# The first pair's q and k in one transfer each, put in order on the chip

## The chip, the cores and the metric

The kernel runs on one NeuronCore of a Trainium2 chip. The metric is the device time of one execution in microseconds, inputs and outputs in HBM; the median of three runs counts. A second, profiled execution gives the trace that is read here.

## The reference

The program is three blocks in a row, all in float32: causal attention over 2 x 12 heads with 448 tokens and a head size of 64, a channel-mixing FFN whose weights come as float64, and a gated FFN with a convolution over the hidden features, also with float64 weights. The change touches only the loading of the first q and k:

```python
scores = scale * np.matmul(q, k.transpose(0, 1, 3, 2))      # q, k, v: (2, 12, 448, 64)
scores = np.where(causal_mask, -1e9, scores)
attn = softmax(scores)                                       # max subtracted, + 1e-9 below
x = np.matmul(attn, v)                                       # heads side by side: (2, 448, 768)
x = rwkv_ffn(x, mu_k, mu_r, w_k, w_v, w_r)                   # token shift, relu^2, sigmoid gate
out = conv_ffn(x, w_in, conv_w, w_out)
```

## The kernel before, in words

Attention goes by pairs of heads, 12 jobs (class `Job`). A pair's raw tile has, on partitions 0 to 63, q and, on 64 to 127, k: seven chunks of 64 tokens, partition p of chunk c holding token 64 c + p, both heads side by side (`half`, line 210). So a partition's tokens lie 64 apart in HBM and each transfer of one head is 448 pieces of 256 B. `Lk` (lines 300 to 306) issues the q halves on SP and, for pair 0 and for pairs from 4 on, the k halves: pair 0's from ScalarE's queue. For pairs 1 to 3 GpSimd issues k (`Lp`). Pair 0's second q half is issued by GpSimd ahead of everything else (line 212).

`kqT` (line 322) turns the chunks on TensorE: 7 transposes for q and 7 for k, chunk c to columns 64 c to 64 c + 63 of a PSUM bank. `kC` copies the two banks to SBUF as qT and kT. `sc` multiplies them to scores, `red` subtracts the mask and takes the row extreme on VectorE, `exp` is on ScalarE, `norm` mostly on GpSimd, `T_`, `C` and `V` bring the probabilities to v.

The order on TensorE, VectorE, ScalarE and GpSimd is written out by hand in the string `ORDER` (line 527): each token such as `0:kqT` or `0:kC.q/v` issues its instructions in program order on its engines, a letter behind the slash naming the engine. Transfers on SP keep the order in which the tokens issue them. `W0` and `W*n` are dummy matmuls of 128 x 128 on a tile of ones (`keep_warm`, line 589); each shows as two passes in the trace. `sm:L` loads small parameters on SP (`mu_k`, `mu_r`, `conv_w`); `sm:a` takes the absolute value of the raw `conv_w` on ScalarE, the first ACTIVATE of the kernel; `sm:n` does four small VectorE steps. `w1:L` loads the first slice of a weight matrix.

Raw weights have two buffers (`raws`, line 111). `turn` takes the next free buffer and puts it at the end of the list again: the dummy operand `warm` takes the first one, so that the list stands at the second when slice 1 asks for one. A buffer is written again only when all readers of the tile that had it are done.

Later stages (`xr_products`, the pk, pv and ph products) follow in `ORDER` and in a stretch that a planner orders; they read nothing that the change touches.

Of the kernel before, what the change touches and what calls it, by code (L numbers as in the profile page):

```python
# [9 lines left out]
F32 = mybir.dt.float32  # L10
# [9 lines left out]
def kernel(  # L20
# [18 lines left out]
    nc = tc.nc  # L39
    B, H, S, D = q.shape  # L40
    P = 128
    WT = 3 * P
    LO = P // 2
# [34 lines left out]
    def copy(eng, out_, in_):  # L78
        (nc.vector.tensor_copy if eng == "v" else nc.scalar.copy)(out_, in_)  # L79
# [31 lines left out]
    raws = Slots(wp, "wraw", 2, [P, NF * P], I64)  # L111
# [6 lines left out]
    def in_order(ins):  # L118
        if pinned[0]:
            tc.keep_in_program_order(ins)  # L120
# [86 lines left out]
    first_qk = qks.get(0, "rqk_0")  # L207

    def half(x, b, h):
        return x[b, h].rearrange("(c p) d -> p c d", p=LO)  # L210

    nc.gpsimd.dma_start(out=first_qk[:LO, :, 1], in_=half(q, 0, 1))
    warm = raws.turn("warm").bitcast(F32)[:, :P]
    nc.vector.memset(warm, 1.0)
    ident = smp.tile([P, P], F32, tag="ident", name="ident", bufs=1)
    make_identity(nc, ident)

# [2 lines left out]
    for r in (slice(0, LO), slice(LO, P)):  # L220
        nc.gpsimd.affine_select(
            out=mask[r, MAIN:], in_=mask[r, MAIN:], compare_op=ALU.is_ge,
# [9 lines left out]
    def home(tag):  # L232
        return act if tag in early else late[0]

    def big(tag, name):
        return home(tag).tile([P, 2, NT], F32R, tag=tag, name=name)
# [8 lines left out]
    def width(t):  # L245
        return t.stop - t.start
# [4 lines left out]
    def bank(key, uses):  # L251
        tag = free.pop(0)
        t = ps.tile([P, 512], F32, tag=tag, name=key, bufs=1)
        held[key] = [tag, t, uses]
        return t

    def used(key):
        h = held[key]
        h[2] -= 1
        if not h[2]:  # L260
            free.append(h[0])
        return h[1]

    NQ = S // LO
# [21 lines left out]
    class Job:  # L286
# [12 lines left out]

        def Lk(self):  # L300
            self.raw = first_qk if self.i == 0 else qks.get(self.i, self.name("rqk"))
            for j in range(2):
                if self.i or j == 0:
                    in_order(nc.sync.dma_start(out=self.raw[:LO, :, j], in_=half(q, self.b, 2 * self.hp + j)))
            if self.i not in (1, 2, 3):
                self.k_half(nc.sync if self.i else nc.scalar)

        def Lp(self):
            self.k_half(nc.gpsimd)
# [12 lines left out]
        def kqT(self, _):  # L322
            t = self.raw
            pt = {n: bank(self.name(n), 1) for n in "qk"}
            for c in range(NQ):
                for n, r in (("q", slice(0, LO)), ("k", slice(LO, P))):
                    nc.tensor.transpose(
                        pt[n][:, c * LO:(c + 1) * LO], t[r, c].rearrange("p h d -> p (h d)"), ident[r, r]
                    )
            qks.put(self.i)  # L330

        def kC(self, eng, n):
# [125 lines left out]
    def products(out_, w, x, t, n, c):  # L458
        o = slice(c * P, c * P + P)
        mm3(out_, w[0][:, 0, o], w[0][:, 1, o], x[c][:, 0, t], x[c][:, 1, t], c == 0, c == n - 1)  # L460
# [21 lines left out]
    def first_steps(s):  # L482

        if s == "L":
            t = act.tile([P, 4 * P], F32, tag="U2", name="small")
            small["m"] = mr = t[:2 * NC, :P]
            in_order(nc.sync.dma_start(out=mr[:NC], in_=mu_k.rearrange("(c p) -> c p", p=P)))
            in_order(nc.sync.dma_start(out=mr[NC:], in_=mu_r.rearrange("(c p) -> c p", p=P)))
            small["r"] = cr = t[:3 * NF, 2 * P:]
            in_order(nc.sync.dma_start(out=cr.bitcast(I64), in_=conv_w.rearrange("t (f p) -> (t f) p", p=P)))  # L490
            small["c"] = t[:3 * NF, P:2 * P]
        elif s in "an":
            for x in "a" if s == "a" else "bcde":
                narrow(x, small["c"], small["r"].bitcast(I32))
        elif s == "T":
            pm = bank("small", 1)
            nc.tensor.transpose(pm[:, :2 * NC], small["m"], ident[:2 * NC, :2 * NC])
            nc.tensor.transpose(pm[:, P:P + 3 * NF], small["c"], ident[:3 * NF, :3 * NF])
        else:
            pm = used("small")  # L500
            nc.vector.tensor_copy(mu[:, :2 * NC], pm[:, :2 * NC])
            nc.vector.tensor_scalar(mu[:, 2 * NC:4 * NC], mu[:, :2 * NC], -1.0, 1.0, ALU.mult, ALU.add)
            nc.vector.tensor_copy(cw, pm[:, P:P + 3 * NF])

    class Slice:
# [19 lines left out]
                wcs.put(e)  # L525

    ORDER = """
        W0 W*2 0:Lk sm:L sm:a 0:kqT W*2 0:kC.q/v sm:n W*1 0:kC.k/a 0:sc.2 0:red.2 0:exp.2 0:red.3 1:Lk 1:Lp 2:Lk
        2:Lp pads 0:red.0 1:kqT 0:sc.1 1:kC.q/v 1:kC.k/a 1:sc.2 0:red.5 0:red.1 1:sc.1 0:exp.0 0:red.6 0:exp.3
        0:exp.5 0:red.4 1:red.3 0:exp.1 1:red.2 3:Lk 3:Lp 0:exp.6 4:Lk 0:exp.4 2:kqT 1:red.5 2:kC.q/v 2:kC.k/a  # L530
        w1:L 0:rec 0:norm.6/p 0:norm.1/p 1:red.0 1:exp.5 0:norm.5/p 1:exp.0 0:norm.0/p 0:norm.4/p 1:red.6
# [57 lines left out]
    def keep_warm(n):  # L589
        for _ in range(n):  # L590
            nc.tensor.matmul(ones[:, :P], warm, warm, start=True, stop=True)

    def xr_products(e, b, c):
        if c == 0:
            bank(f"pr{e}_{b}", 1)
        t = PART[b]
        products(held[f"pr{e}_{b}"][1][:, :width(t)], [slices[e].t], xr, t, NC, c)
        xr_done[e] += 1
        if xr_done[e] == B * NC:
            whls.put(e)  # L600

    def keep_sr(e, b, eng):
        if e not in sr:
            sr[e] = home(f"U{e}").tile([P, NT], F32, tag=f"U{e}", name=f"sr{e}")
        t = PART[b]
        copy(eng, sr[e][:, t], used(f"pr{e}_{b}")[:, :width(t)])

    def xk_step(x, s, eng):
        b, c = divmod(x, NC)
        if s == "H":  # L610
            mix_h(xk[c], mixed[c][:, b], b, eng)
        else:
            mix_l(xk[c], mixed[c][:, b], b, eng)
# [4 lines left out]
    def issue(token):  # L618
        what, _, eng = token.partition("/")
        if what == "W0":  # L620
            keep_warm(7)
        elif what == "pads":
            for z in pads:
                nc.gpsimd.memset(z, 0.0)
        elif what == "Wend":
            used("W")
        elif what[:2] == "W*":
            keep_warm(int(what[2:]))
        elif what == "act2":
            actx.close()  # L630
            late.append(ctx.enter_context(tc.tile_pool(name="act2", bufs=1, reuse_waits="tile")))
            for c in (1, 4, 0, 2, 5, 3):
                xk[c] = big(f"X{c}", f"xk{c}")
            for e in (4, 5, 3):
                sr[e] = home(f"U{e}").tile([P, NT], F32, tag=f"U{e}", name=f"sr{e}")
        elif what[0] == "E":
            f, b = divmod(int(what[1:]), B)
            t = PART[b]
            pk_banks[f, b] = bank(f"pk{f}_{b}", 1)[:, :width(t)]
            for c in range(NC):  # L640
                products(pk_banks[f, b], [slices[NE + f].t], [xk[i] for i in range(NC)], t, NC, c)
        elif what[:2] == "pr":
            xr_products(*(int(y) for y in what[2:].split(".")))
        elif what[:2] == "sr":
            keep_sr(*(int(y) for y in what[2:].split(".")), eng)
        else:
            who, op = what.split(":")
            if who == "sm":
                first_steps(op)
            elif who[0] == "w":  # L650
                slices[int(who[1:])].step(op, eng)
            elif who[0] == "k":
                xk_step(int(who[1:]), op, eng)
            else:
                op, *a = op.split(".")
                job = jobs[int(who)]
                if op in ("Lk", "Lp", "Lv"):
                    getattr(job, op)()
                else:
                    getattr(job, "T_" if op == "T" else op)(eng, *a)  # L660

    ET = mybir.EngineType
    with tc.manual_schedule(engines={ET.PE, ET.Activation, ET.DVE, ET.Pool}):
        for token in ORDER.split():
            issue(token)
# [58 lines left out]
    for f in range(NF):  # L724
# [3 lines left out]
        for t, pk in pks:  # L728
            a = mslots.turn(f"a{f}")[:, :t.stop - t.start]
# [8 lines left out]
    for e in range(NE):  # L738
# [3 lines left out]
        for t, pv in token_mm(f"pv{e}", w, k2, e == 0):  # L742
            a = mslots.turn(f"xv{e}")[:, :t.stop - t.start]
# [358 lines left out]
```

## Time and profile before

| | |
|---|---|
| median of three runs | 353.47 us (353.36 to 353.78) |
| profiled execution | 353.09 us |
| its span, first to last instruction | 351.3 us |
| TensorE busy | 344.4 us, 98% |
| VectorE busy | 308.8 us, 88% |
| ScalarE busy | 223.4 us, 64% |
| GpSimd busy | 96.0 us, 27% |

Times within the trace count from the first instruction. In the trace PE is TensorE's matmul and PEld its weight load, DVE is VectorE, ACT ScalarE, POOL GpSimd and SP SyncE; a q behind a name is its instruction queue, where a transfer's issue stands. TensorE's ends are modelled, so that neighbours overlap in the timeline.

### The profile page before, as it was taken

What the parts mean: (1) busy time and instruction counts of PE and PEld (TensorE: products, weight loads), DVE (VectorE), ACT (ScalarE), POOL (GpSimd) and SP (SyncE); (2) the same over time, 40 slices, a digit from 0 to 9 for tenths busy, and PEclk for the clock granted to TensorE, in tenths of its full rate; (3) what the DMA queues carried; (4) which work ended last, traced back from release to release, by engine and by line L of the source; (5) the groups of instructions that cost most, each with busy time, mean ns of one, the idle gap of its engine ahead of it and who ended that gap; (6) DMA issues with size and microseconds to landing.
All of it is one profiled execution on the core that took longest, in us unless ns stands there. A gap on an engine that the chain in (4) does not pass through costs nothing.

```text
span 351.3 us, 7223 instructions
## 1 busy us (share of the span) xinstructions
PE 344.4 (98%) x2682; PEld 307.0 (87%) x2682; DVE 308.8 (88%) x645; ACT 223.4 (64%) x502; POOL 96.0 (27%) x153
## 2 busy tenths in 40 slices
PE   8899999999999999999999999999999999999995
PEld 7678787888888898988898999998888999999995
DVE  3999999999999988889988998888997999888731
ACT  3999999999300067777795354346657868757501
POOL 8577988973814000000000000000000000368000
PEclk9999999999999999999999999999999999999999
DMA  7955693531422424554627244544241200389523
GB/s 184 242 131 133 139 259 67 144 118 32 150 90 91 129 64 168 179 211 145 214 93 238 90 135 136 174 139 138 90 125 56 90 2 0 67 141 221 115 90 135
DMA packets 60320, 45.33 MB, mean 129 GB/s; under 512 B 31608, under 2 KB 59036, under 8 KB 60284
## 3 DMA queue, kind: packets, MB, share of 16 engines
q1 hardware_dynamic: 56140, 39.90, 37.4%
q0 software_dynamic: 3216, 4.74, 7.2%
q8 instruction: 21, 0.34, 0.4%
q10 hardware_dynamic: 928, 0.23, 0.3%
q14 instruction: 15, 0.12, 0.1%
HBM read 38.17 MB, written 2.75 MB: 117 GB/s over the span
## 4 chain that ended last, share of the span: by engine, by line
PE 88%; DVE 4%; ACT 4%; POOL 2%; issue 1%; POOLq 0%; ACTq 0%
PE pk L66 17%; PE pv L66 17%; PE pr L66 13%; PE A L66 7%; PE po L418 4%; PE B L66 4%; PE s L348 3%; ACT p L370 3%; PE c L66 2%; PE D L66 2%; DVE e L361 2%; PE Yb L390 1%; PE ph5l L66 1%; PE ph4l L66 1%; PE ph6l L66 1%; PE ph7l L66 1%
## 5 line engine op out<-in xcount | busy, mean ns | idle before, releaser
L925 POOL DMA_DIRECT2D s<-g x12 | 12.7, 1179 | 191.3 <-ACT st L87 185.1
L370 ACT ACTIVATE p<-e,st 128x128 f32<-128x128 f32 (+6 forms) x84 | 43.0, 528 | 1.8 <-DVE st L361 1.8
L72 POOL TENSOR_SCALAR p<-p,st 128x384 f32<-128x384 f32 (+6 forms) x70 | 36.4, 538 | 14.3 <-DVE st L361 4.4
L361 DVE CUSTOM_DVE_ANT_0 e<-s,mask 128x128 f32<-128x128 f32 (+6 forms) x84 | 31.7, 413 | 0.5 <-PE s L348 0.5
L730 ACT ACTIVATE a<-pk 128x384 f32<-128x384 f32 (+1 forms) x16 | 8.5, 534 | 35.8 <-PE pk L66 35.8
L418 PE MATMUL po<-pt,v 128*64 128x128 f32 (+4 forms) x384 | 23.8, 277 | 0.0
L348 PE MATMUL s<-kT,qT 64*64 64x448 f32 (+6 forms) x336 | 22.5, 386 | 0.6 <-ACT p L370 0.3
L418 PEld LDWEIGHTS po<-pt,v 128*64 128x64 f32 x384 | 20.0, 137 | 3.4 <-ACT pt L79 0.2
L845 DVE SCALAR_TENSOR_TENSOR cv<-hT,cw,cv 128x448 f32<-128x448 f32 x32 | 21.5, 679 | 1.3 <-ACT cv L842 1.3
L348 PEld LDWEIGHTS s<-kT,qT 64*64 64x64 f32 x336 | 14.5, 132 | 6.6 <-ACT kT L79 0.6
L370 ACT ACTIVATION_READ_ACCUMULATOR p<-e,st 128x1 f32 x84 | 18.2, 217 | 0.0
L87 ACT ACTIVATE x<-xv 128x512 fp32r<-128x512 f32 (+1 forms) x12 | 6.8, 577 | 9.0 <-DVE xv L744 8.9
L91 DVE TENSOR_TENSOR k<-a,k 128x384 fp32r<-128x384 f32 (+1 forms) x16 | 9.8, 619 | 1.6 <-ACT k L87 1.6
L849 ACT ACTIVATE cv<-cv 128x448 f32<-128x448 f32 x16 | 9.1, 571 | 3.2 <-DVE cv L845 3.2
L842 ACT ACTIVATE cv<-hT,cw 128x448 f32<-128x448 f32 x16 | 10.7, 668 | 0.5 <-DVE g L91 0.3
L851 DVE TENSOR_TENSOR cv<-cv,hT 128x448 f32<-128x448 f32 x16 | 9.9, 619 | 1.2 <-ACT cv L849 1.2
L1037 ACT ACTIVATE o<-A 128x384 f32<-128x384 f32 x3 | 1.5, 491 | 14.7 <-PE A L66 14.6
L66 PE MATMUL pv<-k,wv0hl 128*128 128x512 f32 (+1 forms) x48 | 9.9, 364 | 0.0
L925 POOL DMA_DIRECT2D wo6raw<-g x8 | 8.8, 1153 | 3.9 <-ACT wo6raw L950 3.9
L66 PE MATMUL pv<-k,wv2hl 128*128 128x512 f32 (+1 forms) x48 | 9.8, 363 | 0.0
L66 PE MATMUL pv<-k,wv5hl 128*128 128x512 f32 (+1 forms) x48 | 9.8, 363 | 0.0
L66 PE MATMUL pv<-k,wv3hl 128*128 128x512 f32 (+1 forms) x48 | 9.8, 363 | 0.0
(520 smaller groups left out, 1102.9 us busy)
## 6 DMA issues: line engine op xcount, KB each, us to landing
rqk<-in_q_dram SPq DMA_DIRECT2D x23, 112.0 KB, 3.2
v<-in_v_dram SPq DMA_DIRECT2D x24, 96.0 KB, 3.2
s<-g POOLq DMA_DIRECT2D x12, 192.0 KB, 4.2
rqk<-in_k_dram SPq DMA_DIRECT2D x16, 112.0 KB, 3.0
wo6raw<-g POOLq DMA_DIRECT2D x8, 192.0 KB, 4.7
wv0raw<-in_moe_w_v_dram SPq DMA_DIRECT2D x1, 1024.0 KB, 4.6
wv1raw<-in_moe_w_v_dram SPq DMA_DIRECT2D x1, 1024.0 KB, 4.7
wv2raw<-in_moe_w_v_dram SPq DMA_DIRECT2D x1, 1024.0 KB, 4.8
```

The lines of the kernel that those rows point to most:

```text
L66: nc.tensor.matmul(ps_out, x, y, start=first and i == 0, stop=last and i == 2, skip_group_check=more,)
L72: nc.gpsimd.tensor_scalar(out_, in_, s, 1.0, ALU.mult, ALU.mult)
L91: e.tensor_tensor(out_, x, f32(h), ALU.subtract)
L348: nc.tensor.matmul(held[self.name(f"s{f}")][1][h, o:z], qT[r, i * LO:(i + 1) * LO], kT[r, :(i + 1) * LO], start=True, stop=True,)
L361: nc.vector.tensor_tensor_reduce(t[:, :w], used(self.name(f"s{f}"))[:, o:z], mask[:, S - w:], -SCALE, 3e38, ALU.add, ALU.min, self.st[:, 0 ...
L370: nc.scalar.activation(p[:, :w], self.s[i][:, :w], AF.Exp, bias=self.st[:, 0, i:i + 1], scale=-1.0, accum_out=self.st[:, 1, i:i + 1],)
L418: nc.tensor.matmul(self.T["po"][j * D:(j + 1) * D, 1 + i * LO - z:1 + (i + n) * LO], self.v[:, kc, j], self.T["pt"][:, a - z:a + n * LO], ...
L842: nc.scalar.activation(a, x[:, 0:S], AF.Copy, scale=cw[:, f:f + 1])
L845: nc.vector.scalar_tensor_tensor(a, x[:, j:S + j], cw[:, j * NF + f:j * NF + f + 1], a, ALU.mult, ALU.add)
L849: nc.scalar.activation(a, a, AF.Sigmoid)
L851: (nc.gpsimd if eng == "p" else nc.vector).tensor_tensor(a, a, hc, ALU.mult)
L925: nc.gpsimd.dma_start(out=dst, in_=f32(x), accum_op=ALU.add)
```

## The change

Pair 0's q and k come in one transfer each, both heads together, q from SP and k from ScalarE. Partition p gets the seven tokens 7 p to 7 p + 6, which lie in a row in HBM, so that a piece is 7 x 64 x 4 = 1792 B. They land in a staging tile with the heads one behind the other. VectorE copies chunks 0 to 3 and ScalarE chunks 4 to 6 to the raw tile, heads side by side. Chunk c then holds the tokens 7 p + c, and the transposes of pair 0 write to every seventh column from c on, so that the banks hold the tokens in order. GpSimd's transfer at the start is gone. `0:Lk` stands first in `ORDER`; there are 5 dummy matmuls in `W0` instead of 7, and a `W*2` ahead of the transposes is gone. The staging tile takes its turn in the raw-weight buffers, behind `warm`.

```diff
-    nc.gpsimd.dma_start(out=first_qk[:LO, :, 1], in_=half(q, 0, 1))
     warm = raws.turn("warm").bitcast(F32)[:, :P]
     nc.vector.memset(warm, 1.0)
+    stage = raws.turn("stage").bitcast(F32)[:, :2 * S].rearrange("p (j c d) -> p j c d", j=2, c=S // LO)
...
         def Lk(self):
             self.raw = first_qk if self.i == 0 else qks.get(self.i, self.name("rqk"))
+            if self.i == 0:
+                self.whole_rows()
+                return
             for j in range(2):
-                if self.i or j == 0:
-                    in_order(nc.sync.dma_start(out=self.raw[:LO, :, j], in_=half(q, self.b, 2 * self.hp + j)))
-            if self.i not in (1, 2, 3):
-                self.k_half(nc.sync if self.i else nc.scalar)
+                in_order(nc.sync.dma_start(out=self.raw[:LO, :, j], in_=half(q, self.b, 2 * self.hp + j)))
+            if self.i > 3:
+                self.k_half(nc.sync)
+
+        def whole_rows(self):
+            for x, r, e in ((q, slice(0, LO), nc.sync), (k, slice(LO, P), nc.scalar)):
+                in_order(e.dma_start(
+                    out=stage[r].rearrange("p j c d -> p j (c d)"),
+                    in_=x[0, :2].rearrange("j (p c) d -> p j (c d)", p=LO),
+                ))
+            for e, cs in (("v", slice(0, 4)), ("a", slice(4, NQ))):
+                copy(e, self.raw[:, cs], stage[:, :, cs].rearrange("p j c d -> p c j d"))
...
-                    nc.tensor.transpose(
-                        pt[n][:, c * LO:(c + 1) * LO], t[r, c].rearrange("p h d -> p (h d)"), ident[r, r]
-                    )
+                    cols = slice(c * LO, (c + 1) * LO) if self.i else slice(c, S, NQ)
+                    nc.tensor.transpose(pt[n][:, cols], t[r, c].rearrange("p h d -> p (h d)"), ident[r, r])
...
-        W0 W*2 0:Lk sm:L sm:a 0:kqT W*2 0:kC.q/v sm:n W*1 0:kC.k/a 0:sc.2 0:red.2 0:exp.2 0:red.3 1:Lk 1:Lp 2:Lk
+        0:Lk W0 sm:L sm:a 0:kqT W*2 0:kC.q/v sm:n W*1 0:kC.k/a 0:sc.2 0:red.2 0:exp.2 0:red.3 1:Lk 1:Lp 2:Lk
...
         if what == "W0":
-            keep_warm(7)
+            keep_warm(5)
```

## Rows read from the trace of the kernel before

**Rows 1.** Window 20 to 89 us: busy us per engine (instructions), granted clock, DMA share, GB/s

```profile
20.00:89.00 69.00, 68.17 (x1123) 56.62 (x1119) 67.59 (x217) 68.49 (x205) 52.45 (x82) 1.00 0.51 132
```

**Rows 2.** Timeline, 0 to 5 us: start, us, engine, line, operation, tiles, count, idle before

```profile
0.74 0.72 SPq L304 DMA_DIRECT2D rqk<-in_q_dram  x1
0.74 1.66 ACTq L313 DMA_DIRECT2D rqk<-in_k_dram  x2
1.06 4.21 PE L591 MATMUL W<-warm 128*128 128x128 f32 x18 [1.06 <-DVE warm L214]
1.29 0.91 POOL L212 DMA_DIRECT2D rqk<-in_q_dram  x1 [0.85 <-POOLq L1086]
...
2.43 1.28 ACT L140 ACT_TABLE_LOAD   x1 [2.43 <-issue]
...
2.76 6.87 SPq L304 DMA_DIRECT2D rqk<-in_q_dram  x8
...
3.59 2.85 POOL L313 DMA_DIRECT2D rqk<-in_k_dram  x4
4.83 0.31 ACT L140 ACTIVATE small<-small 24x128 f32<-24x128 f32 x1 [1.12 <-DMA small<-in_moe_conv_w_dram]
```

**Rows 3.** First pair's transfers from issue to landing: q's head 0; k's head 1

```profile
DMA to landing us min/median/max: 2.6/2.6/2.6
...
L313 ACTq DMA_DIRECT2D rqk<-in_k_dram x1: 909/909/909, 1.5 to 1.5; - x1
...
DMA to landing us min/median/max: 3.5/3.5/3.5
```

**Rows 4.** Timeline, 5.2 to 8 us

```profile
5.20 0.34 PE L327 MATMUL q<-ident,rqk 64*128 64x64 f32 x1
...
5.94 0.62 DVE L79 COPY qT<-q 128x448 f32<-128x448 f32 x1 [4.94 <-PE k L327]
5.97 0.54 ACT L79 COPY kT<-k 128x448 f32<-128x448 f32 x1 [0.83 <-PE k L327]
...
6.48 0.42 DVE L143 TENSOR_SCALAR small<-small 24x128 f32<-24x128 f32 x1
...
6.71 0.99 PE L348 MATMUL s<-kT,qT 64*64 64x384 f32 x16
...
7.63 0.27 PE L327 MATMUL q<-ident,rqk 64*128 64x64 f32 x1
...
7.87 0.36 DVE L361 CUSTOM_DVE_ANT_0 e<-s,mask 128x192 f32<-128x192 f32 x1
```

**Rows 5.** DMA queues, 0 to 12 us and 130 to 140: packets, MB, share of engines

```profile
q10 hardware_dynamic: 928, 0.23, 8.5%
...
q1 hardware_dynamic: 928, 1.57, 48.2%
```

**Rows 6.** Groups by shape, VectorE and ScalarE: count, busy us, mean ns, idle before

```profile
L85 DVE CAST xk<-mixed 128x448 fp32r<-128x448 f32 x5 | 2.1, 429 | 0.0
...
L87 ACT ACTIVATE st<-s 128x384 fp32r<-128x384 f32 x9 | 4.5, 510 | 0.0
```

**Rows 7.** Dummy passes before 5 us and after 6 (ns min/median/max); window 2 to 3

```profile
L591 PE MATMUL W<-warm x18: 421/421/582, 1.1 to 4.8; 128*128 128x128 f32 x18
...
L591 PE MATMUL W<-warm x10: 275/275/377, 5.8 to 12.1; 128*128 128x128 f32 x10
...
2.00:3.00 1.00, 1.00 (x7) 1.00 (x6) 0.00 (x0) 0.57 (x1) 0.99 (x4) 1.00 0.82 189
```

**Rows 8.** Slice 1's load, the last dummy passes; its landing and first reader

```profile
11.03 0.62 SPq L162 DMA_DIRECT2D wr1raw<-in_moe_w_r_dram  x1
...
11.66 0.71 PE L591 MATMUL W<-warm 128*128 128x128 f32 x4
...
L138 DVE TENSOR_SCALAR wr1c<-wr1raw x1: 552/552/552, 20.1 to 20.1; 128x768 int32<-128x768 int32 x1
...
DMA to landing us min/median/max: 6.0/6.0/6.0
```

## The prediction

> **What bounds the kernel now.** I read the windows first, then the timeline of the first 14 us, then single transfers, and last the shapes. From 20 to 89 us TensorE, VectorE and ScalarE are each busy for all but 1.4 us of 69 [rows 1]: whatever starts there earlier or later ends earlier or later by as much, and what follows is TensorE almost without a gap. So the change is worth what it moves the start of that stretch, no more. It touches only the first 13 us, and there the reader is to find what is late at each step.
>
> Up to 5.2 us everything waits for the first pair's data. Four transfers of 112 KB bring it: SP and ScalarE issue one each at 0.74, GpSimd one at 1.29, ScalarE its second behind its first [rows 2]. The first, q's head 0, lands 2.6 us after its issue, at 3.3; the last, k's head 1, issued at 1.5, lands 3.5 later, at 5.0 [rows 3]. TensorE does 18 dummy passes from 1.06 to 5.27 and starts the transposes at 5.20 [rows 2, 4]: filler and data end together. VectorE, idle for 4.94 us until 5.94, is from then on a chain without a gap: copy of qT, conversion of the small parameters, first reduction at 7.87 [rows 4]. The scores that it reads start at 6.71, after ScalarE's copy of kT (5.97 to 6.51).
>
> The profiled execution took 353.09 us, 351.3 of span and 1.8 around it; the median of the runs is 353.47. I add the terms up against 353.09 and put the difference, 0.38, back on at the end. About 0.2%, 0.71 us, is what a measurement of this kernel can tell from no change.
>
> **The change part by part.**
>
> *Transfers.* Two instead of four, both issued at 0.74, the same bytes in 256 packets of 1792 B instead of 1792 packets of 256 B. A 256 B packet takes 0.085 x 16 x 12 us / 928 = 17.6 ns of one DMA engine; the nearest row for large ones, a stretch of weight loads with 1.57 MB in 928 packets (1.69 KB each on average), gives 0.482 x 16 x 10 us / 928 = 83 ns [rows 5], so 88 ns for 1792 B. The 16 engines are then kept for 256 x 88 / 16 = 1.41 us instead of 1.97. When is the last byte there? Not before the 3.3 of the first transfer, not after today's 5.0. That first transfer needed 448 x 17.6 / 16 = 0.49 us of the engines; adding the other 0.92 to 3.3 gives 4.2, less what it already shared with k's packets. I take 4.0, that is 1.0 earlier than now, and keep 3.5 and 4.7 as ends.
>
> *Copies.* New work ahead of the transposes; both wait for q and for k, as they span all 128 partitions. ScalarE copies 384 elements a partition: the row of that size from SBUF to SBUF has 510 ns. VectorE copies 512: 429 ns for 448 gives 0.49 [rows 6]. Both engines were idle there. Price 0.55 with the hand-over, ends 0.45 and 0.8 (GpSimd issues transfers beside it, and VectorE's conversion of only 128 elements at 6.48 took 0.42 while GpSimd was at work [rows 4]). Transposes can start at 4.6 instead of 5.2.
>
> *Dummy passes.* Four matmuls fewer ahead of the transposes, 10 passes instead of 18. At 4.21 / 18 = 0.23 us each they end at 3.4 and hold nothing up; TensorE then pauses for about 1.2 us, which it did not do before.
>
> *Transposes.* The same 14 instructions into other columns; now 0.74 us from 5.20 to VectorE's start at 5.94 [rows 4]. No row shows a write with seven columns between neighbours; it costs between nothing and as much again, and I take nothing, as the columns written are as many. But the transposes now come before 5.3, and there the clock is the lower one: a dummy pass lasts 421 ns before 5 us and 275 after 6 [rows 7]. [...] With a factor of up to 1.5 on 0.74 I take 1.0, and the transposes end at 5.6, 0.34 earlier than now. (Ends: 5.0 and 6.3.)
>
> *ScalarE's queue.* This is the step that I think decides. Now the table load (1.28 us) runs at 2.43, in idle time, directly ahead of the first ACTIVATE, the absolute value of the small parameters at 4.83 [rows 2]. The copies of line 79 show as COPY, another operation, and one of them is now queued ahead. If the load stays tied to that ACTIVATE, it comes behind the copy, which waits for data: copy 4.0 to 4.53, load to 5.81, absolute value (0.31) to 6.12, copy of kT (0.54) to 6.66 instead of 6.51. The scores then start at 6.86, 0.15 later than now. VectorE copies qT from 5.6 to 6.2, has its four small steps to do (6.48 to 7.87 now, so 1.39), and is ready at 7.6; the scores' bank is ready about 0.9 after their start, at 7.76. First reduction 7.76 instead of 7.87: 0.1 is left of 0.34. [...]
>
> *GpSimd* loses its transfer at 1.29 (0.91 us), so identity, mask and pair 1's k, at 3.59 now, come some 0.9 earlier. Pair 1's transposes follow the scores at once (6.71 + 0.99 = 7.70, against 7.63 [rows 4]), so I count no gain; it removes a limit that a larger gain would meet.
>
> *SP* issues as before: q at 0.74, the small parameters, the run of eight from 2.76 [rows 2]. One thing moves: the staging tile takes the second raw-weight buffer in turn, so slice 1's load gets the first, in which the dummy operand lies, and must wait for the last dummy passes (11.66 to 12.37) instead of going at 11.03 [rows 8]. Behind it on SP are pair 5's loads and the first v. It lands 6.0 after its issue, 18.4 instead of 17.1, and is first read at 20.1: hidden with 1.7 to spare, cost nothing; without that cover it would be up to 1.3.
>
> Sum: 0.1 if the first reduction is what counts, 0.34 if later steps recover the transposes' lead; I take 0.2. 353.09 - 0.2 + 0.38 gives **353.25**, its own range 352.9 to 353.6.
>
> **Rivals.**
>
> *The load is not late: faster.* If it goes ahead of the copy, it is done by 1.5 + 1.3 = 2.8. ScalarE then copies kT at 5.6 and the scores start 0.34 earlier; with the data at 3.5 and the copies at their lower end, 0.9 earlier. 352.5 to 353.1, middle 352.8. For it: today's load waits for nothing, and GpSimd's head start keeps pair 1 from stopping it. Against: it stands next to its ACTIVATE.
>
> *The clock rises late: slower.* TensorE now works without a pause from 1.06 until the passes get short; with a pause from 3.4 to 4.6 the full clock may come later. This decides from the start of the scores at 6.9, as the dummies and transposes before it have slack. The scores' 0.99 us becomes nearly 2 and the first reduction 8.7 instead of 7.87, 0.8 lost; pair 1's transposes and the next scores add up to 0.5 more: 354.3 to 354.8, and 354.3 with some slack. For it: TensorE is 99% busy from 20 to 89 us [rows 1], so lost time does not come back. Against: the dummies and the transposes still fill most of the time. [...]
>
> *It doesn't do what it says: slower.* The two transfers land at 4.7, as the bytes are the same, and the copies come on top: transposes end at 6.3 rather than 5.94, and with the table load behind the copy, kT's copy at 7.4. That is 0.4 to 0.8 slower, 354.1.
>
> **Chances.** Forecast 0.42, load not late 0.32, clock late 0.18, late landing 0.08. Faster by over 0.2% (under 352.76): two thirds of the second case and a sixth of the forecast's, where the data is early, 0.28. Slower (over 354.18): most of the third case, half of the fourth and the forecast's far tail, 0.22. No change 0.50. Range for 8 in 10: 352.4 to 354.4.
>
> **What would show it.** Right: two transfers for the first pair with some 3.2 us to landing, ACT_TABLE_LOAD behind a COPY of 384 elements that ends near 4.5, the first reduction near 7.75, SP's slice load near 12. Wrong, to the fast side: the load at 1.5 and scores before 6.4. Wrong, to the slow side: dummy passes of 421 ns behind the transposes and scores of 2 us; or landings beyond 4.5.

## The result and the profile after

The changed kernel takes 356.81 us (median of six runs, 356.23 to 356.93) beside 353.62 (six runs, 353.14 to 354.13) for the kernel before on the same chip: ratio 1.0091, 95% interval 1.0079 to 1.0104, some 3.2 us slower. Its profiled execution took 356.8 us with a span of 355.0, against 353.09 and 351.3.

The first timeline is that of the changed kernel, columns as in [rows 2]; it answers to [rows 2] and [rows 4].

```profile
0.74 0.71 ACTq L312 DMA_DIRECT2D stage<-in_k_dram  x1
...
0.74 0.73 SPq L312 DMA_DIRECT2D stage<-in_q_dram  x1
...
1.06 2.50 PE L601 MATMUL W<-warm 128*128 128x128 f32 x10 [1.06 <-DVE warm L213]
...
5.15 1.28 ACT L79 ACT_TABLE_LOAD   x1 [5.15 <-DMA stage<-in_q_dram]
5.18 0.68 DVE L79 COPY rqk<-stage 128x512 f32<-128x512 f32 x1 [4.18 <-DMA stage<-in_q_dram]
...
6.00 0.34 PE L339 MATMUL q<-ident,rqk 64*128 64x64 f32 x1 [2.44 <-DVE rqk L79]
...
6.45 0.51 ACT L79 COPY rqk<-stage 128x384 f32<-128x384 f32 x1
...
7.01 0.37 PE L339 MATMUL q<-ident,rqk 64*128 64x64 f32 x1 [0.32 <-ACT rqk L79]
...
7.52 1.65 PE L601 MATMUL W<-warm 128*128 128x128 f32 x6
7.63 0.62 DVE L79 COPY qT<-q 128x448 f32<-128x448 f32 x1 [1.77 <-PE q L339]
7.67 0.53 ACT L79 COPY kT<-k 128x448 f32<-128x448 f32 x1 [0.49 <-PE q L339]
...
9.10 1.77 PE L358 MATMUL s<-kT,qT 64*64 64x384 f32 x16
10.80 0.36 PE L339 MATMUL q<-ident,rqk 64*128 64x64 f32 x1
...
11.04 0.36 DVE L371 CUSTOM_DVE_ANT_0 e<-s,mask 128x192 f32<-128x192 f32 x1 [1.78 <-PE s L358]
```

Read it from the top. The dummies end at 3.56 and TensorE idles for 2.44 us, until 6.00. The data is complete at 5.08 (q; k came at 4.17), no earlier than before. ScalarE's table load stands between the landing and its copy, so the last transposes wait until 7.01. Then come six dummy passes, still long: 1.65 us where such a group takes 0.94 at the full clock (e2, below). The scores start at 9.10, though kT was ready at 8.20, and take 1.77 us where [rows 4] have 0.99. The first reduction is at 11.04 instead of 7.87: 3.17 us late, nearly all of the loss.

The chain of waits of the changed kernel (start, us, what) has the same steps; 1.58 us of dummy passes stand on it, between transposes and scores. In the kernel before, the scores start 0.20 us after kT is ready (6.51 to 6.71 [rows 4]); here it is 0.90:

```profile
0.74 4.34 DMA stage<-in_q_dram
...
5.15 1.28 ACT L79
6.45 0.52 ACT rqk L79
...
7.59 1.58 PE W L601 x6
9.17 1.69 PE s L358 x10
```

The windows of the changed kernel (columns as in [rows 1]) show that the column of granted clock says 1.00 here too, as in [rows 7], and so can't be used; what tells of the clock is the length of equal instructions (the median dummy pass takes 421 ns up to 8.7 us and 275 from 15.2 on). By the first clock record in each trace TensorE has its full clock from 12.6 us on, and from 5.4 in the kernel before. The second row answers to [rows 1]: the stretch from 20 to 89 us is as full as it was, so nothing lost ahead of it comes back.

```profile
6.00:13.00 7.00, 6.68 (x66) 5.21 (x70) 3.42 (x14) 3.25 (x10) 2.15 (x11) 1.00 0.51 129
...
20.00:89.00 69.00, 67.90 (x1119) 55.97 (x1121) 67.62 (x226) 68.45 (x212) 54.92 (x85) 1.00 0.53 133
```

### The profile page after: what moved, and what is told of

It reads as the page before. It is cut to its first block, busy times and chain, and to the rows that moved or that the text cites. A ratio compares the mean times of both kernels' runs of the same rounds, so it can differ in the third digit from the quotient of the medians.

```text
span 355.0 us, 7205 instructions
## 1 busy us (share of the span) xinstructions
PE 345.4 (97%) x2674; PEld 307.4 (87%) x2674; DVE 309.5 (87%) x646; ACT 224.1 (63%) x503; POOL 95.8 (27%) x152
## 4 chain that ended last, share of the span: by engine, by line
PE 89%; DVE 6%; ACT 2%; DMA 1%; issue 1%; ACTq 0%
PE pk L66 16%; PE pv L66 16%; PE pr L66 13%; PE A L66 7%; PE po L428 4%; PE s L358 4%; PE B L66 4%; DVE e L371 2%; PE c L66 2%; PE D L66 2%; DMA stage<-in_q_dram 1%; PE Yb L400 1%; PE ph5l L66 1%; PE ph4l L66 1%; PE ph6l L66 1%; PE ph7l L66 1%
## 5 line engine op out<-in xcount | busy, mean ns | idle before, releaser
L358 PE MATMUL s<-kT,qT 64*64 64x448 f32 (+6 forms) x336 | 23.5, 402 | 0.5 <-DVE pt L79 0.3
L358 PEld LDWEIGHTS s<-kT,qT 64*64 64x64 f32 x336 | 15.3, 138 | 6.7 <-issue 1.2
L339 PE MATMUL q<-ident,rqk 64*128 64x64 f32 x84 | 8.9, 245 | 2.8 <-DVE rqk L79 2.4
L339 PEld LDWEIGHTS q<-ident,rqk 64*128 64x128 f32 x84 | 6.9, 150 | 4.5 <-issue 2.9
L66 PE MATMUL pv<-k,wv4hl 128*128 128x512 f32 (+1 forms) x48 | 9.8, 363 | 0.0
```

Of the source, the lines that this page charges most:

```text
L66: nc.tensor.matmul(ps_out, x, y, start=first and i == 0, stop=last and i == 2, skip_group_check=more,)
L339: nc.tensor.transpose(pt[n][:, cols], t[r, c].rearrange("p h d -> p (h d)"), ident[r, r])
L358: nc.tensor.matmul(held[self.name(f"s{f}")][1][h, o:z], qT[r, i * LO:(i + 1) * LO], kT[r, :(i + 1) * LO], start=True, stop=True,)
```

## The experiments

Theory C: TensorE's pause keeps the clock at its lower level for longer, and that is most of the loss; the rest is copies behind a landing that is no earlier. Theory L: the late table load is most of it. Ten kernels ran, each group of them beside the kernel before (its medians: 353.18 with e1 to e4, 353.24 with e5 to e8, 353.04 with e9 and e10). The table has medians, ratios to the kernel before with 95% intervals (taken over all runs, so not exactly the quotients of the medians), and times from the one profiled execution of each kernel: last landing of the first pair's data, first transpose, first scores, first reduction, start of the pr products (the first matmuls on xr, in the stretch from 20 to 89 us), and full clock from the trace's first clock record.

| kernel | us | ratio | landed | transp. | scores | red. | pr | clock |
|---|---|---|---|---|---|---|---|---|
| before | 353.62 | | 4.99 | 5.20 | 6.71 | 7.87 | 52.92 | 5.4 |
| after | 356.81 | 1.0091 [1.0079, 1.0104] | 5.08 | 6.00 | 9.10 | 11.04 | 56.53 | 12.6 |
| e1_load_early | 356.29 | 1.0079 [1.0057, 1.0100] | 5.13 | 6.00 | 8.52 | 10.45 | 55.88 | 11.9 |
| e2_no_pause | 354.70 | 1.0036 [1.0024, 1.0048] | 5.13 | 6.04 | 7.49 | 8.65 | 53.71 | 6.0 |
| e3_both | 354.40 | 1.0035 [1.0022, 1.0048] | 4.92 | 5.98 | 7.43 | 8.58 | 53.66 | 5.8 |
| e4_before_pause | 355.15 | 1.0054 [1.0037, 1.0072] | 5.11 | 4.83 | 7.72 | 9.66 | 55.40 | 11.8 |
| e5_no_copies | 353.11 | 0.9998 [0.9989, 1.0006] | 5.27 | 5.20 | 6.75 | 7.91 | 52.96 | 5.2 |
| e6_by_head | 353.41 | 1.0002 [0.9990, 1.0015] | 4.86 | 5.20 | 7.31 | 8.46 | 53.51 | 6.8 |
| e7_q_on_sp | 353.10 | 0.9999 [0.9988, 1.0011] | 5.08 | 5.20 | 7.01 | 8.17 | 53.23 | 6.2 |
| e8_short_pause | 354.56 | 1.0039 [1.0024, 1.0054] | 4.97 | 5.58 | 7.15 | 8.30 | 53.95 | 3.9 |
| e9_no_wait | 353.03 | 0.9994 [0.9985, 1.0003] | 4.90 | 4.35 | 6.57 | 7.72 | 52.77 | 5.3 |
| e10_copies_by_head | 353.51 | 1.0017 [1.0006, 1.0027] | 4.43 | 5.21 | 6.95 | 8.10 | 53.16 | 5.9 |

### The pause and the load

**e1_load_early**, the changed kernel with the load drawn at once:

```diff
+            nc.scalar.activation(first_act, warm[:, :1], AF.Abs)
             for e, cs in (("v", slice(0, 4)), ("a", slice(4, NQ))):
```

> The changed kernel with one more ScalarE instruction ahead of the copies, an absolute value of one element a partition, which draws the table load to the start; nothing else. In the changed kernel's trace the load runs from 5.15 to 6.44, behind q's landing at 5.08, and ScalarE's copy ends at 6.96. Theory L (the late load is most of the 3.2 us): the copy ends near 5.7, the transposes near 6.6 instead of 7.6, and the time is 354.6 to 355.4. Theory C (the late clock is most of it): the first reduction stays behind TensorE at the lower clock, and the time is 355.9 to 356.6. In both the load is at 1.5.

The load goes to 1.48, the transposes finish without a wait, and the pr products start 0.65 us earlier; the median falls by about 0.5. The clock stays low to 11.9. In both executions q is the last to land, so the two differ in little but the load: it is a small part.

**e2_no_pause**, the changed kernel with the pause filled:

```diff
         if what == "W0":
-            keep_warm(5)
+            keep_warm(11)
```

> The changed kernel with 11 dummy matmuls at the start instead of 5, so that TensorE is busy from 1.06 to about 5.8, nothing else. Theory C: the full clock comes before 7.5 instead of at 12.6, the scores' 1.8 us become 1.0, and the time is 354.6 to 355.4. Theory L: the scores still cannot start before 8.3 (transposes 7.6, copies 0.62), so at most the 0.8 us by which the dummies behind the transposes now delay the scores go, and the time is 355.9 to 356.5.

With dummy work alone some 60% of the loss is gone by the ratios, and 2.82 of 3.61 us at the pr products. In the timeline of this kernel the passes behind the transposes take 0.94 us and the scores follow at 7.49. One more thing differs from the changed kernel's execution: here q lands first (4.22) and k last (5.13), and ScalarE, which waits for q first, has its load done earlier:

```profile
4.29 1.28 ACT L79 ACT_TABLE_LOAD   x1 [4.29 <-DMA stage<-in_q_dram]
...
5.15 0.43 DVE L79 COPY rqk<-stage 128x512 f32<-128x512 f32 x1 [4.15 <-DMA stage<-in_k_dram]
...
5.58 0.51 ACT L79 COPY rqk<-stage 128x384 f32<-128x384 f32 x1
...
6.62 0.94 PE L601 MATMUL W<-warm 128*128 128x128 f32 x6
```

**e3_both** has both edits.

> The changed kernel with the early load and the 11 dummy matmuls together. What is left is the landing of q at 5.1 (k's head 1 at 5.0 before the change) and the copies, 0.7 to 0.8: transposes at 5.9 instead of 5.2. If landing, load and clock are the whole cause, 354.0 to 354.5; if something else of the change costs (the strided transposes, the later loads), over 354.8.

The pr products start with it at 53.66, in e2 at 53.71. That doesn't show that the load is hidden as soon as the pause is gone, as e2's execution had q first; with q last, as in the changed kernel and in e3, the load would end near 6.4 and hold the last transposes up (until 7.01 in the changed kernel). What e3 does show, beside e1, where q is last too and the load as early, is the pause: 55.88 less 53.66, 2.22 us.

**e4_before_pause** puts the pause alone into the kernel before, with no copies, no staging tile and the load where it was:

```diff
-        W0 W*2 0:Lk sm:L sm:a 0:kqT W*2 0:kC.q/v
+        W0 0:Lk sm:L sm:a 0:kqT W*2 0:kC.q/v
...
         if what == "W0":
-            keep_warm(7)
+            keep_warm(5)
```

> The kernel before with 5 dummy matmuls ahead of the first transposes instead of 9, so that TensorE pauses from 3.4 to 5.2 and nothing else moves. Theory C: the clock rises only after the pause, beyond 8, and the time is 354.3 to 355.3. If the pause is harmless (theory L): 353.4 to 353.9, as before, with the rise near 5.4.

2.0 us slower (355.15 against 353.18). Its timeline is the test of the mechanism: the transposes come as early as 4.83, and the first reduction comes at 9.66, 1.79 us late.

```profile
1.06 2.50 PE L591 MATMUL W<-warm 128*128 128x128 f32 x10 [1.06 <-DVE warm L214]
...
4.83 0.34 PE L327 MATMUL q<-ident,rqk 64*128 64x64 f32 x1 [1.27 <-DMA rqk<-in_q_dram]
...
6.15 1.65 PE L591 MATMUL W<-warm 128*128 128x128 f32 x6
...
7.72 1.77 PE L348 MATMUL s<-kT,qT 64*64 64x384 f32 x16
...
9.66 0.36 DVE L361 CUSTOM_DVE_ANT_0 e<-s,mask 128x192 f32<-128x192 f32 x1 [1.74 <-PE s L348]
```

**e8_short_pause** is the changed kernel with `keep_warm(9)`.

> The changed kernel with 9 dummy matmuls in W0 in place of 5: TensorE's pause ahead of pair 0's transposes is about 0.8 us in place of 2.4, copies and late table load unchanged. Theory C graded (the clock rises the later the longer the pause): full clock between 6 and 12 us, 355.0 to 355.9. Theory C all or none: either as with the pause filled, full clock by 6.5 and 354.5 to 355.0, or as the changed kernel, full clock near 12.5 and 356.2 to 356.9. Rival L (the late table load sets the time): 356.2 to 356.9 with the full clock by 6.5.

Neither theory's number settles it. The profiled execution had its full clock at 3.9, while the dummies still ran (they end at 4.66); the pause of 0.92 us after that cost nothing visible, and scores and transposes ran short. Its first reduction is only 0.43 us late, and yet it took 354.65 us: at 55 us VectorE waits 1.11 us for weight slice 3 (issued at 51.07, 46.05 in the kernel before, and landed at 56.06), and the step that reads it, with GpSimd at work from 55.72, takes 1.20 us. In e2 the same step waits for nothing and takes 0.62. First e8, then e2:

```profile
56.09 1.20 DVE L138 TENSOR_SCALAR wr3c<-wr3raw 128x768 int32<-128x768 int32 x1 [1.11 <-DMA wr3raw<-in_moe_w_r_dram]
```

```profile
55.23 0.62 DVE L138 TENSOR_SCALAR wr3c<-wr3raw 128x768 int32<-128x768 int32 x1
```

So this one number holds a loss that is neither theory's. The slice lands 3.4 us ahead of its reader in the kernel before and 0.37 ahead in e5; SP issues it behind a long row of other transfers, and whether the change makes it late more often was not tested. The twelve runs spread from 353.59 to 356.21, four of them above 355.3. Whether in those the full clock came only after the pause, or the slice came later still, was not traced and stays open.

### The copies and the landing

**e5_no_copies**, with `keep_warm(9)`, leaves the copies out; pair 0's transposes read the staging tile:

```diff
-            for e, cs in (("v", slice(0, 4)), ("a", slice(4, NQ))):
-                copy(e, self.raw[:, cs], stage[:, :, cs].rearrange("p j c d -> p c j d"))
...
+                    x = t[r, c].rearrange("p h d -> p (h d)")
+                    if self.i == 0:
+                        x = stage[r].rearrange("p j c d -> p (j c d)")[:, 2 * c * D:2 * (c + 1) * D]
+                    nc.tensor.transpose(pt[n][:, cols], x, ident[r, r])
```

> The changed kernel with 9 dummy matmuls in W0 in place of 5 (they end near 5.2 us) and without the two copies: pair 0's transposes read the staging tile directly, 128 neighbouring elements of one head in place of 64 of each head, so the putting in order is left out and pair 0's values are not the reference's; instructions and bytes are the same otherwise. Theory C (clock, and copies behind a landing that is no earlier): transposes start at the last landing, near 5.15, at the full clock, first scores near 6.7, and the time is that of the kernel before, 353.0 to 353.7. Rival M (the 1.2 us that stay with the pause and the late table load gone come from the middle of the kernel, from the staging tile's buffer or the later slice load): transposes near 5.15 all the same, time 354.1 to 354.7.

The time of the kernel before, step for step up to the scores: transposes into every seventh column 5.20 to 5.94, scores 6.75, and the two large transfers, GpSimd's early start and the later slice load are all still in it. With the pause filled and the copies left out nothing of the loss remains. Its timeline:

```profile
5.20 0.27 PE L340 MATMUL q<-ident,stage 64*128 64x64 f32 x1
...
5.94 0.62 DVE L79 COPY qT<-q 128x448 f32<-128x448 f32 x1 [4.94 <-PE k L340]
...
6.75 0.99 PE L359 MATMUL s<-kT,qT 64*64 64x384 f32 x16
```

At the pr products the copies cost 0.75 us (53.71 less 52.96), by the ratios of e2 and e5 (1.0036 and 0.9998) 1.3. One thing that can add to a late start shows in e3. Here are the timelines of e3 and then of e2 about 67 us: a VectorE step of seven elements a partition, done in 0.17 us in e2, takes 0.85 in e3, where it starts 0.01 us after a GpSimd step of 0.83 and ends 0.03 after it. In e2 GpSimd starts 0.08 after it.

```profile
67.04 0.85 DVE L389 TENSOR_SCALAR st<-st 128x7 f32<-128x7 f32 x1
...
67.03 0.83 POOL L143 TENSOR_SCALAR wr3c<-wr3c 128x768 f32<-128x768 f32 x1
```

```profile
66.87 0.17 DVE L387 TENSOR_SCALAR st<-st 128x7 f32<-128x7 f32 x1
...
66.95 0.83 POOL L143 TENSOR_SCALAR wr3c<-wr3c 128x768 f32<-128x768 f32 x1
```

That is 0.5 us at the pk products (121.81 in e3, 121.36 in e2), from a VectorE step that comes 0.17 later. e1 has the same pair, GpSimd's step at 69.26 and VectorE's at 69.27 (0.84); in its trace only 0.1 us of the 0.65 is left in the span (354.9 against 355.0). Why VectorE's step takes longer there, no row shows. e2's six runs lie at 353.95 (the profiled one), 354.24 and four times near 354.7. The longer step alone is too small for the four: e3, which has it, took 354.38. That q landed last in them, with the load exposed, would fit as well; only profiled executions have a trace, so this stays open.

**e6_by_head** is e5 with four transfers in place of two, one a head:

```diff
-                in_order(e.dma_start(
-                    out=stage[r].rearrange("p j c d -> p j (c d)"),
-                    in_=x[0, :2].rearrange("j (p c) d -> p j (c d)", p=LO),
-                ))
+                for j in range(2):
+                    in_order(e.dma_start(
+                        out=stage[r, j].rearrange("p c d -> p (c d)"),
+                        in_=x[0, j].rearrange("(p c) d -> p (c d)", p=LO),
+                    ))
```

> As e5_no_copies, and q and k in two transfers each, one a head, in pieces of 1792 B, q from SP and k from ScalarE (putting in order left out here too). Theory S (a transfer lands late after its last packet because of the large pieces): the last landing stays near 5.1 and the time within 0.2 of e5_no_copies. Rival Q (two large transfers keep too few of the 16 DMA engines busy, or are started late as a whole): heads 0 land near 3.3, the last one by 4.5, TensorE still has dummies to 5.2, scores at most 0.1 us earlier, time within 0.3 of e5_no_copies; the landings tell the theories apart, not the time.

Heads 0 land at 3.21 and 3.60, heads 1 at 4.66 and 4.86: between the theories. In two transfers the last landing lies between 4.90 and 5.27 in seven traces, so 4.86 is at most a small gain. The time is the same; its scores at 7.31 come behind dummy passes that were still long (1.24 us for six), with the full clock only at 6.8.

**e7_q_on_sp**, the kernel before with GpSimd's transfer on SP:

```diff
-    nc.gpsimd.dma_start(out=first_qk[:LO, :, 1], in_=half(q, 0, 1))
...
-                if self.i or j == 0:
+                if True:
```

> The kernel before with one edit: GpSimd's transfer of q's head 1 goes to SP, behind head 0; nothing is copied, the dummies are those of before. GpSimd is then free 0.9 us earlier, as in the changed kernel. Theory C: that relief is worth nothing by itself, as pair 1's k is not what the first transposes of pair 1 wait for: 353.0 to 353.8. Rival G (GpSimd's start is a limit of the kernel before): pair 1 and the stretch from 20 us on come 0.3 to 0.6 earlier, 352.6 to 353.0. Rival D (four transfers on two queues land later): last landing near 5.6 and 353.8 to 354.3.

No difference: GpSimd's relief is worth nothing by itself, and two queues bring four transfers about as soon as three did (5.08 and 4.99).

**e9_no_wait**: e5's edit with `x = warm[r]` and `keep_warm(7)`: the transposes wait for no transfer.

> The changed kernel with 7 dummy matmuls in W0 in place of 5 (they end near 4.35 us), without the copies, and with pair 0's transposes reading the tile of ones instead of the data, so that they wait for no transfer; the two transfers are still made. Pair 0's values are not the reference's. It asks what the sought gain would be worth if the data came 0.9 us earlier. Theory E (the first reduction sets the time, one to one): transposes 4.35 to 5.35 at the lower clock, scores near 6.1, first reduction near 7.2 in place of 7.87, time 352.5 to 352.9. Rival F (pair 1's data, VectorE's small steps or a later clock take it back): scores near 6.1 all the same, pair 1's transposes not before 7.5, time 353.0 to 353.6.

What could the sought gain have been worth? With transposes 0.85 us earlier the scores come 0.14 earlier and the time is not measurably better. The timeline names what stops it: ScalarE's copy of kT stands behind the absolute value of the small parameters, which waits for its own transfer until 5.79 (4.83 in the kernel before [rows 2]). Pair 1's transposes then wait for their own data until 7.76.

```profile
4.35 0.37 PE L340 MATMUL q<-ident,warm 64*128 64x64 f32 x1
...
5.39 0.62 DVE L79 COPY qT<-q 128x448 f32<-128x448 f32 x1 [4.39 <-PE k L340]
5.79 0.32 ACT L140 ACTIVATE small<-small 24x128 f32<-24x128 f32 x1 [3.02 <-DMA small<-in_moe_conv_w_dram]
...
6.01 0.50 ACT L79 COPY kT<-k 128x448 f32<-128x448 f32 x1
...
6.57 0.99 PE L359 MATMUL s<-kT,qT 64*64 64x384 f32 x16 [0.34 <-ACT kT L79]
...
7.76 0.24 PE L340 MATMUL q<-ident,rqk 64*128 64x64 f32 x1 [0.21 <-DMA rqk<-in_q_dram]
```

**e10_copies_by_head**: e6's transfers and `keep_warm(9)`, with the copies by head:

```diff
-            for e, cs in (("v", slice(0, 4)), ("a", slice(4, NQ))):
-                copy(e, self.raw[:, cs], stage[:, :, cs].rearrange("p j c d -> p c j d"))
+            for j in range(2):
+                for e, r in (("v", slice(0, LO)), ("a", slice(LO, P))):
+                    copy(e, self.raw[r, :, j], stage[r, j])
```

> The changed kernel with 9 dummy matmuls in W0 in place of 5, q and k in two transfers each (one a head, pieces of 1792 B), and the copies by head: VectorE copies q, ScalarE k, each as soon as its own transfer lands, so that only the copy of the last head stands behind the last landing (4.7 to 4.9, as in e6_by_head). Theory C (clock and copies are the whole loss): the table load stands behind the first copy's wait, near 3.3 to 4.5, hidden; last copy 4.9 to 5.4, transposes 5.45, scores near 7.0, time 353.3 to 353.9: no better than the kernel before. Rival W (copies of 64 partitions take twice as long, or the clock rises late in the pause of 0.2 us): transposes after 5.8, 354.2 to 355.0. Rival B (the change can win in this form): transposes before 5.2, under 352.9.

The best form of the change: by the ratios 2.6 us better than the one given, still 0.06% to 0.27% slower than the kernel before. The first copies hide behind the second transfers; TensorE goes from dummies to transposes without a pause. The load did not come where I expected it: here, where each copy waits for one transfer only, it stands at 1.98, ahead of the wait. Its timeline:

```profile
1.98 1.28 ACT L79 ACT_TABLE_LOAD   x1 [1.98 <-issue]
...
3.27 0.56 ACT L79 COPY rqk<-stage 64x448 f32<-64x448 f32 x1
...
4.46 0.61 DVE L79 COPY rqk<-stage 64x448 f32<-64x448 f32 x1 [0.17 <-DMA stage<-in_q_dram]
5.21 0.35 PE L341 MATMUL q<-ident,rqk 64*128 64x64 f32 x1
```

No kernel was measurably faster than the kernel before.

## Why the prediction was wrong

The forecast was 353.25 us with a range of 352.4 to 354.4; the kernel took 356.81. (The sum as written, 353.09 - 0.2 + 0.38, is 353.27; the slip plays no part.)

**The bound** was right for this kernel: 3.17 us lost at the first reduction are 3.61 at the pr products and 3.7 in the span. It is not exact: in e3 and e8 the first reduction is 0.71 and 0.43 us late and the span 1.3 and 1.6 longer, by waits of the later stretch itself.

**Dummy passes: "they end at 3.4 and hold nothing up".** This is the step that failed. They end at 3.56, and what they did was not filler: without them the full clock comes at 11.8 to 12.6 us in three kernels (after, e1, e4) in place of 3.9 to 6.8 in the nine others, and the pause alone costs 2.0 us (e4). Rival 2 had the mechanism and its sign, at 18%. It was priced at 0.8 to 1.3 us, because I counted from the start of the scores on; the dummy passes behind the transposes, which I gave slack, took 1.65 us and stood on the path. No run shows the factor of two by which the scores' 0.99 us was to become nearly 2: at the lower clock they took 1.77 (after, e4), and a dummy pass 421 ns against 275 [rows 7]. Measured, the pause is worth 2.0 us in e4's time and 2.22 at the pr products between e1 and e3. The "against", that dummies and transposes still fill most of the time, rested on a pause of 1.2 us, and e4, with a pause of 1.27, had its full clock at 11.8 all the same. How the pause holds the clock back, no run here shows.

**Transfers: "I take 4.0".** Also failed: 5.08, beyond my end of 4.7. The reasoning took the engines' time as what ends the transfer, 1.41 us in place of 1.97. In the DMA view from 0 to 6 us, first of the kernel before and then of the changed one, ScalarE's queue (packets, MB, share of 16 engines) keeps the engines for almost as long:

```profile
q10 hardware_dynamic: 928, 0.23, 17.0%
```

```profile
q10 hardware_dynamic: 144, 0.23, 15.1%
```

Less than a sixth of the packets, 11% less time: 0.91 us, where my 88 ns a packet give 0.70 for this half of the data. And the trace has one landing for each transfer: the tile's summary in the changed kernel, over the two, has

```profile
DMA to landing us min/median/max: 3.4/3.9/4.3
```

so the first 224 KB come at 4.17, the second at 5.08, and each copy needs both. Which of the two is first changes: k in four traces of this form, q in three (e2, e5, e8).

**Copies: 0.55.** About right for each (0.43 to 0.68 and 0.51), but behind a landing that is no earlier they are a loss of about 0.7 us at the pr products, where I had a gain.

**Transposes.** Seven columns apart cost nothing that shows (0.74 us in e5 as in [rows 4]), and 1.0 us at the lower clock was right (e1: 6.00 to 7.01).

**ScalarE's queue.** Right that a load of 1.28 us comes late, wrong in the place: the copy itself draws it. Where that copy waits for two transfers the load stands behind the first wait and ahead of the copy (5.15 in after; 4.08 in e8, after q's landing at 4.01 and ahead of k's at 4.97). In both the load bears the copy's line, L79, and the COPY comes before the first ACTIVATE (6.45 and 6.87 in after; 5.38 and 5.80 in e8): a COPY is enough to draw it. It cost 0.65 us at the pr products in this kernel, where q landed last (e1). That is less than a fifth of the loss, so it did not decide.

**GpSimd** no gain (e7), and **SP**'s slice load late but hidden, both right for slice 1; slice 3's load was not hidden in e8. Slice 1's goes at 15.9 instead of 11.03 [rows 8], since the last dummies are later too, lands 4.5 later at 20.4, and is read at 23.7; the tile's summary in the changed kernel:

```profile
L162 SPq DMA_DIRECT2D wr1raw<-in_moe_w_r_dram x1: 421/421/421, 15.9 to 15.9; - x1
L138 DVE TENSOR_SCALAR wr1c<-wr1raw x1: 553/553/553, 23.7 to 23.7; 128x768 int32<-128x768 int32 x1
...
DMA to landing us min/median/max: 4.5/4.5/4.5
```

**The cases.** I treated the clock, the late landing and the late load as alternatives and let the range end at the price of one. They add up at the pr products (q lands last in all of these but e5, which has no copy for the load to hold up): the early load gives back 0.65 us (56.53 to 55.88, e1), filling the pause 2.22 more (to 53.66, e3), and without the copies the start is that of the kernel before (52.96, e5, and 52.92): 0.70 for copies and landing. Together that is 3.57 of the 3.61. Rivals 2 and 3 together, by my own prices (0.8 to 1.3 and 0.6 over 353.47), give 354.9 to 355.4, outside the range already.

## What to carry to other kernels

Dummy work ahead of the first real matmuls can be part of the path (2.0 us in e4): whoever shortens it, or makes the data later, should fill the gap up to the data, and price the lower clock over everything until the full one returns, dummy passes included (six of them took 1.65 us in place of 0.94, the scores 1.77 in place of 0.99). A rearranging copy pays only if the landing moves by more than the copy (here 0.43 to 0.68 us behind a landing at 5.08 in place of 4.99); compare landings, not packet counts or engine time. Before moving a start forward, ask what stands behind it: in e9 the wait for the small parameters left 0.14 us of 0.85.

## What the hardware showed unexpectedly

The moment of the full clock varies between profiled executions whose dummies begin alike at 1.06 us, from 3.9 (e8) to 6.8 (e6); two kernels that differ by a few tenths of a us need several runs for that alone. So does the order in which two transfers issued together land. Neither fewer transfers nor larger pieces brought 448 KB clearly earlier: 4.86 to 5.27 in eleven traces, 4.43 in e10. A VectorE step of seven elements took 0.84 to 0.85 us in place of 0.17 where GpSimd's step of 0.83 started 0.01 us ahead of it (e1, e3).
